# Attention into a gated feed-forward layer on one core: weights loaded in thirds, output buffers moved, more load buffers, the last output row block split

## The chip, the cores and the metric

The kernel runs on one NeuronCore of a Trainium2 chip. Its time is the device time of one execution in microseconds. Four executions of the kernel before took 388.49, 388.51, 391.55 and 392.05 us, a median of 390.03 us. A further execution was recorded by the hardware profiler; all durations below come from that one.

TensorE (PE) does the matrix products, with its weight loads listed apart as PEld. VectorE is DVE, ScalarE is ACT, GpSimd is POOL, and SyncE is SP. SP does nothing but issue DMAs here. POOL issues DMAs too, those that change the type on the way.

## The reference

```
scores = q @ k_all^T / 8          # k_all: 16 beacon keys, then 576 keys; causal on the 576
a      = softmax(scores)          # per batch (8) and head (8), 576 queries, D = 64
attn   = a @ v_all
x      = attn as [4608 tokens, 512]
out    = (relu(x @ w_gate) * (x @ w_val)) @ w_out      # d_ff = 1536, output fp32
```

## The kernel before, in words

The work is one long list of steps, written out by hand in `plan`. Instructions are emitted in program order, and each engine runs its own in that order; an instruction that waits holds up all that stand behind it on the same engine. A step of a batch takes two attention units (`Unit`): `qk` writes scores to PSUM, `exp` is done by ACT, and POOL zeroes what the causal mask removes (L353). A chunk of queries whose units are all done gets its values in the next step (`Chunk.av` on PE, `invert` and `scale` on DVE), which writes transposed rows into `xT`. Between attention pieces stands feed-forward work on 512-token tiles (`Ffn`): 12 groups `up` (four gate matmuls L420, ReLU on ACT L423, four value matmuls L429, product on DVE L431) and 4 groups `down` (12 matmuls L436, copy by ACT to an output buffer `ob` L439, and a store on SP L441 that is queued at the start of the next step).

Steps 0 to 6 are batch 0, steps 7 to 10 feed-forward alone (0, 3, 3 and 2 groups), steps 11 to 17 batch 1 with one group each, steps 18 and 19 feed-forward alone (3 groups each), and from step 20 each of batches 2 to 7 takes seven steps. In the code `s2` is 11. The groups of the first tile (four downs among them) are the 8 of steps 8 to 10, the 7 of steps 11 to 17, and the first of step 18.

PSUM has eight banks: `s_ps` two buffers of two banks (scores, and the value product of an `up` when its argument `spare` is true), `f_ps` two buffers of one bank (gate product, value product when `spare` is false, down product), `o_ps` two of one.

Queues matter around the change. POOL issues the weight loads (`load_w`, two DMAs a call), then the second batch's keys and queries (`load_cast_quarter`, eight DMAs), a tiny memset that holds back SP's loads of that batch's values, and later `w_out` in two DMAs (`load_wo`). SP issues everything else: raw fp32 tiles into the `stage` buffers (L231), transposing DMAs of cast tiles (L255) and the stores (L441). For batch 2 and on, `fetch(b, s0, late)` spreads 15 tiles (key, query, value for each of five row blocks) over steps: tile row `j` is loaded at `s0+j`, cast on POOL at `s0+j+late`, transposed by SP one step later. Batch 2 has `s0` = 11 and `late` = 3; batch 3 has `s0` = 20 and `late` = 1. Of the actions of a step, the first half is emitted before the step's feed-forward groups and before the second unit's exp and mask, the rest after them.

At the start PE runs idle matmuls on a memset tile (`warm_up`). At the end, groups left over run one after the other, and SP stores the last 128 rows.

Of the kernel before, what the change touches and what calls it, by code (L numbers as in the profile page):

```python
# [10 lines left out]
FP32 = mybir.dt.float32  # L11
BF16 = mybir.dt.bfloat16
# [141 lines left out]
def kernel(  # L154
# [23 lines left out]
    M_TILE = 512  # L178
# [4 lines left out]


    const = ctx.enter_context(tc.tile_pool(name="const", bufs=1))
    wg = const.tile([P, KM, d_ff], BF16, name="wg")
    nc.vector.memset(wg[:, 0, :M_TILE], 1.0)
    ident = const.tile([P, P], BF16, name="ident")
    make_identity(nc, ident)
    ones = const.tile([P, C], BF16, name="ones")  # L190
    nc.vector.memset(ones, 1.0)
    xT = const.tile([P, KM, n_tokens], BF16, name="xT")
    wv = const.tile([P, KM, d_ff], BF16, name="wv")
    wo = const.tile([P, NF, d_model], BF16, name="wo")
    bounds = [const.tile([P, 256], FP32, name=n) for n in ("least", "most")]
    for x in bounds:
        nc.vector.memset(x, 1.0)

    main = ctx.enter_context(ExitStack())
    kvq = main.enter_context(tc.tile_pool(name="kvq", bufs=2))  # L200
    stage = main.enter_context(tc.tile_pool(name="stage", bufs=8))
    half = main.enter_context(tc.tile_pool(name="half", bufs=6))
    psb = main.enter_context(tc.tile_pool(name="psb", bufs=10))
    nrm = main.enter_context(tc.tile_pool(name="nrm", bufs=7))
    fsb = main.enter_context(tc.tile_pool(name="fsb", bufs=2))
    osb_p = main.enter_context(tc.tile_pool(name="osb", bufs=3))
# [201 lines left out]
    class Ffn:  # L408
# [22 lines left out]
            nc.vector.tensor_mul(self.h[:, nf, c0:c1], gs[:, :n], u[:, :n])  # L431

        def down(self, ms):
            o = f_ps.tile([P, d_model], FP32, name="f")
            for nf in range(NF):
                nc.tensor.matmul(o, self.h[:, nf, ms * P:(ms + 1) * P], wo[:, nf, :],  # L436
                                 start=(nf == 0), stop=(nf == NF - 1))
            ob = osb_p.tile([P, d_model], FP32, name="ob")
            nc.scalar.copy(ob, o)  # L439
            m = self.m0 + ms * P  # L440
            later_sp.append(lambda: nc.sync.dma_start(out[m:m + P, :], ob))  # L441

        def groups(self, c0, c1, d0, d1):
            t = (c1 - c0) * 8 / 2400
# [17 lines left out]
        return cnt  # L462

    ffn_tiles = [Ffn(m * M_TILE) for m in range(n_tokens // M_TILE)]
    later_sp = []
    STEPS = 7

    ALONE = ((0, 3, 3, 2), (3, 3))
    BASE = [STEPS * b + sum(map(len, ALONE[:b])) for b in range(B)]
# [8 lines left out]
    with tc.manual_schedule():  # L478
        batches = {}
        dve, act, pool = nc.vector.tensor_copy, nc.scalar.copy, nc.gpsimd.tensor_copy  # L480
        wide_ctx = ExitStack()
# [8 lines left out]
            x.tails = [x.load_rows(k[x.b, :, 512:]), x.load_rows(q[x.b, :, 512:])]  # L490


        idle_ps = o_ps.tile([P, 256], FP32, name="os")

        def warm_up(count, n):
            for _ in range(count):
                nc.tensor.matmul(idle_ps[:, :n], wg[:, 0, :P], wg[:, 0, :n],
                                 start=True, stop=True)

        first = batches[0] = Batch(0)  # L500
# [7 lines left out]
        load_tails(first)  # L508
        for t in range(2, NKT):
            first.load("v", t)  # L510
        warm_up(8, 256)
        first.turn_rows(first.cast_rows(first.beacon, dve), first.kT[:, :, :Nb], dve)()
        warm_up(4, 256)
        def turn_first(i, g):
            for n in "kq":
                ps = f_ps.tile([P, 2, 2, P], BF16, name="f")
                first.turn_quarter(n, i, g, ps, act if n == "q" and g == 0 else dve)()
                if i == 0 and n == "k":
                    warm_up(2, P)
# [7 lines left out]
        warm_up(5, P)  # L527
        cast_first(0, 1)

        def turn_two(x, i, k_bank):  # L530
# [22 lines left out]
        def after(step, action):  # L553
            later_half.setdefault(step, []).append(action)
# [4 lines left out]
        s2 = BASE[1]  # L559

        def turn_next():
            turn_first(0, 1)
            warm_up(5, P)

        between[0] = turn_next
        mid[0] = lambda: cast_first(1, 0)
# [3 lines left out]
        def turn_last():  # L570
            turn_first(1, 0)
            ps = o_ps.tile([P, 2, 2, 2, P], BF16, name="ab")
            moves = []
            for x, n in enumerate("kq"):
                moves.append(first.turn_quarter(n, 1, 1, ps[:, x], dve))
                warm_up((8, 4)[x], P)
            for move in moves:
                move()
            cast_tails(first, dve)
# [5 lines left out]
        after(2, lambda: load_w(wv, moe_w_val, 0, 512))  # L585
        behind[3] = turn_first_tails
        after(3, lambda: first.cast("v", 4, pool))
        after(3, lambda: load_w(wg, moe_w_gate, 512, 1536))
        after(4, lambda: load_w(wv, moe_w_val, 512, 1536))

        def load_second(i):
            for g in range(2):
# [23 lines left out]
        after(s2 - 2, lambda: turn_small(second))  # L616
        mid[s2 - 1] = lambda: turn_two(second, 0, s_ps)
        between[s2 + 1] = lambda: turn_two(second, 1, f_ps)
        after(s2 + 1, wide_ctx.close)

        def fetch(b, s0, late=1):
            at(s0, lambda: batches.update({b: Batch(b)}))
            for j, u in enumerate(UNITS):
                s = s0 + j // 3
                at(s, lambda u=u: batches[b].load(*u))
                at(s + late, lambda u=u: batches[b].cast(*u, pool))
                if u[0] != "v":
                    at(s + late + 1, lambda u=u: batches[b].turn(*u))

        fetch(2, s2, 3)  # L630
        for b in range(3, B):
            fetch(b, BASE[b] - STEPS)

        spans = [(m, m + M_TILE) for m in range(0, n_tokens, M_TILE)]
# [10 lines left out]
        for s, (b, i, quota) in enumerate(plan):  # L645
            have = max([have] + [t for at_, t in ready.items() if at_ <= s])
            while spans and spans[0][1] <= have:
                t0, t1 = spans.pop(0)
                f = ffn_tiles[t0 // M_TILE]
# [53 lines left out]
            for j, (kind, _, run) in enumerate(mine):  # L703
                if j == 0 and other and (kind == "down" or len(mine) == 1):
                    other.pop().exp()
                ups = kinds.count("up")
                run((b is None and (s, j) != (s2 - 1, len(mine) - 1)) or (ups > 1 and j == (1 if ups > 2 else 0)))
                if j == 0:
                    for c in chunks if b != 1 else []:
                        c.scale()  # L710
                        notes.append(c.note)
                    if b is None and s in mid:
                        mid[s]()
                if other:
                    other.pop().exp()
                if b is None and notes:
                    notes.pop(0)()
# [65 lines left out]
```

## Time and profile before

| what | value |
|---|---|
| median of four executions | 390.03 us |
| the profiled execution's own time | 393.2 us |
| its span on the core | 391.3 us |
| PE busy, share of span | 367.7 us, 94% |
| DVE / ACT / POOL busy | 205.4 / 191.7 / 121.7 us |
| mean granted TensorE clock | 0.995 |
| PE busy from 0 to 26, 26 to 61, 61 to 84, 84 to 386 us | 18.49 of 26, 31.77 of 35, 19.53 of 23, 297.94 of 302 us |
| the same stretches, GB/s moved by DMA | 213, 192, 178, 110 |

The page of the profile divides the span into 40 slices and gives each engine's busy share in tenths. Busy time of PE is not PE at its peak, since matmuls overlap; a stretch without busy time is idle for certain. The timeline lists instructions by start, with the idle time of the engine before and what ended it. A store or load on SP shows how long SP took to issue it, not the transfer itself; the time to its landing stands in the table of DMA issues.

### The profile page before, as it was taken

The page shows a single profiled execution, that of the slowest core. Times are in us where ns is not written, and L with a number is a line of the kernel's source. Part 1 is how long each engine was busy: PE and PEld are TensorE (multiplying, and loading weights), DVE is VectorE, ACT ScalarE, POOL GpSimd, SP SyncE. Part 2 cuts the span into 40 slices and gives each one's busy share as a digit, 9 for nine tenths or more (in the row PEclk, how much of TensorE's full clock was granted, in tenths as well). Part 3 has the DMA queues.
Part 4 walks back from the last instruction along what each step waited for, and adds up shares of the span by engine and source line. Part 5 has one row for each costly group of instructions (what it writes and reads, how often), then busy time and mean ns, then how long its engine had stood idle before and what let it go on. Part 6 is the DMA issues. An engine that isn't in the chain of part 4 may idle for free.

```text
span 391.3 us, 10186 instructions
## 1 busy us (share of the span) xinstructions
PE 367.7 (94%) x4252; PEld 186.6 (48%) x4308; DVE 205.4 (53%) x333; ACT 191.7 (49%) x268; POOL 121.7 (31%) x213
## 2 busy tenths in 40 slices
PE   6768999799999999999999999999999999999994
PEld 4543555334554545445544545454545454444441
DVE  4876476345674566466447653665365644412320
ACT  4843494136655554565546545645465533313321
POOL 1882454315543442254225332334201100000000
PEclk9999999989999999999999999999999999999999
DMA  7999997958968782698258924793200020011002
GB/s 227 204 207 187 187 209 172 180 150 187 190 172 211 148 166 81 161 188 178 66 130 208 172 73 132 188 191 71 96 27 2 2 82 28 0 54 56 0 28 85
DMA packets 145555, 49.84 MB, mean 127 GB/s; under 512 B 133216, under 2 KB 139872, under 8 KB 145504
## 3 DMA queue, kind: packets, MB, share of 16 engines
q1 hardware_dynamic: 137536, 43.37, 48.1%
q0 software_dynamic: 7968, 5.77, 9.9%
q8 instruction: 35, 0.57, 0.6%
q14 instruction: 16, 0.13, 0.1%
HBM read 38.27 MB, written 9.44 MB: 122 GB/s over the span
## 4 chain that ended last, share of the span: by engine, by line
PE 85%; DMA 6%; issue 2%; ACT 2%; SPq 2%; DVE 1%; POOL 1%; ACTq 0%; DVEq 0%
PE f L436 23%; PE f L420 23%; PE s L429 13%; PE f L429 10%; PE s L337 6%; PE ab L386 6%; DMA wo<-in_moe_w_out_dram 3%; PE os L386 2%; DMA raw<-in_k_dram 1%; SPq L231 1%; ACT e L345 1%; DMA wide<-in_q_dram 1%; DMA out_dram<-ob 1%; ACT ob L439 0%; DVE r L394 0%
## 5 line engine op out<-in xcount | busy, mean ns | idle before, releaser
L420 PE MATMUL f<-xT,wg 128*128 128x512 bf16 x407 | 110.0, 382 | 5.7 <-ACT ob L439 2.8
L345 ACT ACTIVATE e<-s 128x1024 bf16<-128x1024 f32 (+2 forms) x112 | 104.3, 965 | 21.9 <-PE s L337 21.8
L423 ACT ACTIVATE g<-f 128x512 f32<-128x512 f32 x108 | 64.6, 598 | 87.7 <-PE f L420 80.9
L353 POOL TENSOR_SCALAR_AFFINE_SELECT e<-e 128x512 bf16<-128x512 bf16 (+2 forms) x80 | 47.1, 600 | 162.6 <-ACT e L345 154.0
L436 PE MATMUL f<-wo,hT 128*128 128x512 bf16 x408 | 94.7, 379 | 2.9 <-issue 1.6
L394 DVE RECIPROCAL r<-os 128x240 f32<-128x240 f32 (+2 forms) x45 | 61.0, 1355 | 39.5 <-PE os L386 39.4
L431 DVE TENSOR_TENSOR hT<-g,s 128x512 bf16<-128x512 f32 x59 | 40.5, 687 | 64.8 <-PE s L429 55.8
L429 PEld LDWEIGHTS <-wv 128*128 128x128 bf16 x432 | 42.4, 98 | 52.8 <-issue 3.0
L420 PEld LDWEIGHTS <-wg 128*128 128x128 bf16 x432 | 40.0, 98 | 52.4 <-issue 7.0
L431 DVE TENSOR_TENSOR hT<-g,f 128x512 bf16<-128x512 f32 x49 | 33.7, 688 | 57.6 <-PE f L429 51.8
L436 PEld LDWEIGHTS <-hT 128*128 128x128 bf16 x432 | 40.3, 98 | 48.1 <-issue 0.8
L429 PE MATMUL s<-xT,wv 128*128 128x512 bf16 x231 | 61.0, 383 | 0.2
L439 ACT COPY ob<-f 128x512 f32<-128x512 f32 x36 | 21.1, 587 | 77.1 <-PE f L436 62.8
L429 PE MATMUL f<-xT,wv 128*128 128x512 bf16 x195 | 50.0, 379 | 0.5 <-ACT qT L284 0.2
L250 POOL CAST half<-raw 128x512 bf16<-128x512 f32 (+2 forms) x60 | 36.4, 627 | 16.9 <-DMA kT<-half 6.7
L386 PE MATMUL ab<-e,v 128*32 128x80 bf16 (+4 forms) x1320 | 38.8, 231 | 2.5 <-issue 1.6
L337 PE MATMUL s<-qT,kT 64*128 64x80 bf16 (+3 forms) x704 | 34.0, 228 | 3.0 <-ACT e L345 1.8
L337 PEld LDWEIGHTS <-kT 64*128 64x128 bf16 x704 | 20.1, 95 | 25.8 <-issue 22.6
L386 PEld LDWEIGHTS <-v 128*32 128x32 bf16 (+1 forms) x1408 | 26.4, 97 | 11.1 <-issue 5.9
L386 PE MATMUL os<-e,ones 128*32 128x240 bf16 (+4 forms) x660 | 31.6, 230 | 0.0
L246 POOL CAST v<-raw 128x512 bf16<-128x512 f32 (+1 forms) x40 | 26.1, 656 | 9.0 <-DMA raw<-in_v_dram 8.7
L399 DVE TENSOR_TENSOR xT<-ab,r 128x480 bf16<-128x480 f32 (+2 forms) x45 | 25.0, 555 | 1.0
(59 smaller groups left out, 126.9 us busy)
## 6 DMA issues: line engine op xcount, KB each, us to landing
out_dram<-ob SPq DMA_DIRECT2D x36, 256.0 KB, 2.3
raw<-in_v_dram SPq DMA_DIRECT2D x24, 256.0 KB, 4.4
raw<-in_q_dram SPq DMA_DIRECT2D x24, 256.0 KB, 4.0
raw<-in_k_dram SPq DMA_DIRECT2D x18, 256.0 KB, 4.1
raw<-in_v_dram SPq DMA_DIRECT2D x8, 224.0 KB, 3.7
wo<-in_moe_w_out_dram POOLq DMA_DIRECT2D x2, 768.0 KB, 11.7
raw<-in_k_dram SPq DMA_DIRECT2D x6, 224.0 KB, 4.1
raw<-in_v_dram SPq DMA_DIRECT2D x8, 160.0 KB, 3.8
```

What stands on the lines that cost most here:

```text
L246: copy(self.v[:n, t].rearrange("p (h a d) -> p h a d", a=2, d=C), raw[:n].rearrange("p (h d a) -> p h a d", a=2, d=C))
L250: copy(h[:n], raw[:n])
L337: nc.tensor.matmul(self.s[:, a, c + j * n:c + (j + 1) * n], self.batch.kT[rows, 2 * g + j, kt * P:(kt + 1) * P], self.batch.qT[rows, 2 * g ...
L345: nc.scalar.activation(e[:, :k * 4 * n].rearrange("p (k a x) -> p a k x", k=k, a=2), self.s[:, :, :k * 2 * n].rearrange("p a (k x) -> p a ...
L353: nc.gpsimd.affine_select(out=cols[:, :, :m], in_=cols[:, :, :m], pattern=[[0, 4], [1, m]], compare_op=ALU.is_ge, fill=0.0, base=base, cha ...
L386: nc.tensor.matmul(o[:, q0 - cq0:q0 - cq0 + n], w, e[:kr, 2 * (hh % 2) + hh // 2], start=(i == 0 and part != 1), stop=(i == self.last), sk ...
L394: nc.vector.reciprocal(self.r[:, :n], self.os[:, :n])
L420: nc.tensor.matmul(g[:, :n], wg[:, ki, nf * P:(nf + 1) * P], x[:, ki], start=(ki == 0), stop=(ki == KM - 1))
L423: nc.scalar.activation(gs[:, :n], g[:, :n], AF.Relu)
L429: nc.tensor.matmul(u[:, :n], wv[:, ki, nf * P:(nf + 1) * P], x[:, ki], start=(ki == 0), stop=(ki == KM - 1))
L431: nc.vector.tensor_mul(self.h[:, nf, c0:c1], gs[:, :n], u[:, :n])
L436: nc.tensor.matmul(o, self.h[:, nf, ms * P:(ms + 1) * P], wo[:, nf, :], start=(nf == 0), stop=(nf == NF - 1))
```

## The change

- `wo` is allocated first and takes the place of `wg` as the memset tile that the idle matmuls read. There are fewer and wider idle matmuls: 8 of 256 columns become 4 of 512, 4 of 256 become 2 of 512, 5 of 128 become 2 of 256, and so on; 38 become 14.
- `w_gate` and `w_val` were loaded as columns 0 to 512 and 512 to 1536. They are now loaded as three parts of 512. The middle parts stay after steps 3 and 4; the last parts come after step 6, ahead of the second batch's keys and queries on POOL.
- `stage` has ten buffers instead of eight.
- The output buffers `ob` were three, in a pool of their own. They are six, in a pool made after step 12, when the pool `wide` has been closed, and they use its space.
- The last 128 output rows are computed, copied and stored in two halves of 256 columns.
- Batch 3 is fetched from step 18 with `late` = 2, instead of step 20 with `late` = 1.
- In steps of feed-forward alone the last group of each step is now run with `spare` false; before, that was so for step 10 only.

```
-    wg = const.tile([P, KM, d_ff], BF16, name="wg")
-    nc.vector.memset(wg[:, 0, :M_TILE], 1.0)
+    wo = const.tile([P, NF, d_model], BF16, name="wo")
+    nc.vector.memset(wo[:, 0], 1.0)
...
-    stage = main.enter_context(tc.tile_pool(name="stage", bufs=8))
+    stage = main.enter_context(tc.tile_pool(name="stage", bufs=10))
...
-    osb_p = main.enter_context(tc.tile_pool(name="osb", bufs=3))
...
         def down(self, ms):
-            o = f_ps.tile([P, d_model], FP32, name="f")
-            for nf in range(NF):
-                nc.tensor.matmul(o, self.h[:, nf, ms * P:(ms + 1) * P], wo[:, nf, :],
-                                 start=(nf == 0), stop=(nf == NF - 1))
-            ob = osb_p.tile([P, d_model], FP32, name="ob")
-            nc.scalar.copy(ob, o)
-            m = self.m0 + ms * P
-            later_sp.append(lambda: nc.sync.dma_start(out[m:m + P, :], ob))
+            last = self.m0 + (ms + 1) * P == n_tokens
+            for n0 in range(0, d_model, 256) if last else (0,):
+                n = slice(n0, n0 + 256) if last else slice(0, d_model)
+                o = f_ps.tile([P, d_model], FP32, name="f")
+                for nf in range(NF):
+                    nc.tensor.matmul(o[:, n], self.h[:, nf, ms * P:(ms + 1) * P], wo[:, nf, n],
+                                     start=(nf == 0), stop=(nf == NF - 1))
+                ob = pools["osb"].tile([P, d_model], FP32, name="ob")
+                nc.scalar.copy(ob[:, n], o[:, n])
+                m = self.m0 + ms * P
+                later_sp.append(
+                    lambda m=m, n=n, ob=ob: nc.sync.dma_start(out[m:m + P, n], ob[:, n]))
...
-        idle_ps = o_ps.tile([P, 256], FP32, name="os")
+        idle_ps = o_ps.tile([P, M_TILE], FP32, name="os")
...
-                nc.tensor.matmul(idle_ps[:, :n], wg[:, 0, :P], wg[:, 0, :n],
+                nc.tensor.matmul(idle_ps[:, :n], wo[:, 0, :P], wo[:, 0, :n],
...
-        after(3, lambda: load_w(wg, moe_w_gate, 512, 1536))
-        after(4, lambda: load_w(wv, moe_w_val, 512, 1536))
+        after(3, lambda: load_w(wg, moe_w_gate, 512, 1024))
+        after(4, lambda: load_w(wv, moe_w_val, 512, 1024))
+        after(6, lambda: load_w(wg, moe_w_gate, 1024, 1536))
+        after(6, lambda: load_w(wv, moe_w_val, 1024, 1536))
...
-        after(s2 + 1, wide_ctx.close)
+
+        def close_wide():
+            wide_ctx.close()
+            pools["osb"] = main.enter_context(tc.tile_pool(name="osb", bufs=6))
+
+        after(s2 + 1, close_wide)
...
         fetch(2, s2, 3)
-        for b in range(3, B):
+        fetch(3, BASE[3] - STEPS - 2, 2)
+        for b in range(4, B):
             fetch(b, BASE[b] - STEPS)
...
-                run((b is None and (s, j) != (s2 - 1, len(mine) - 1)) or (ups > 1 and j == (1 if ups > 2 else 0)))
+                run((b is None and j < len(mine) - 1) or (ups > 1 and j == (1 if ups > 2 else 0)))
```

More of the change, by code (lines that the diff above doesn't have):

```diff
@@ L192 @@
     xT = const.tile([P, KM, n_tokens], BF16, name="xT")
+    wg = const.tile([P, KM, d_ff], BF16, name="wg")
     wv = const.tile([P, KM, d_ff], BF16, name="wv")
-    wo = const.tile([P, NF, d_model], BF16, name="wo")
     bounds = [const.tile([P, 256], FP32, name=n) for n in ("least", "most")]
@@ L464 @@
     ffn_tiles = [Ffn(m * M_TILE) for m in range(n_tokens // M_TILE)]
-    later_sp = []
+    later_sp, pools = [], {}
     STEPS = 7
@@ L510 @@
             first.load("v", t)
-        warm_up(8, 256)
+        warm_up(4, M_TILE)
         first.turn_rows(first.cast_rows(first.beacon, dve), first.kT[:, :, :Nb], dve)()
-        warm_up(4, 256)
+        warm_up(2, M_TILE)
         def turn_first(i, g):
@@ L518, in turn_first @@
                 if i == 0 and n == "k":
-                    warm_up(2, P)
+                    warm_up(1, 256)
         def cast_first(i, g):
@@ L526 @@
         turn_first(0, 0)
-        warm_up(5, P)
+        warm_up(2, 256)
         cast_first(0, 1)
@@ L562, in turn_next @@
             turn_first(0, 1)
-            warm_up(5, P)
+            warm_up(2, 256)
         between[0] = turn_next
@@ L575, in turn_last @@
                 moves.append(first.turn_quarter(n, 1, 1, ps[:, x], dve))
-                warm_up((8, 4)[x], P)
+                warm_up(1, (M_TILE, 256)[x])
             for move in moves:
```

## The prediction

> **What bounds the kernel now.** I read the page's slices first, then the list of waits, then the timeline around the one place where both show a hole.
>
> ```profile
> span 391.3 us, 10186 instructions
> ...
> PE   6768999799999999999999999999999999999994
> ...
> PEclk9999999989999999999999999999999999999999
> ```
>
> PE is full from the third slice on. The two thin places are the first 26 us (attention of batch 0, where little else can run) and one slice near 76 us, followed by the only slice with a lower clock. From 84 us to 386 us PE is busy 297.94 of 302 us, so whatever is done must arrive ahead of 84 us or in the tail; between them it can only move PE's work forward as a block.
>
> ```profile
> ACT ob L439 <- DMA out_dram<-ob: 6.6, 1, 6.6
> ...
> PE f L420 <- ACT ob L439: 2.8, 1, 2.8
> ...
> PE f L436 <- DMA wo<-in_moe_w_out_dram: 0.6, 1, 0.6
> ```
>
> The hole is a full set of output buffers. The fourth copy needs the first buffer back, and its store waited on SP:
>
> ```profile
> 70.96 0.59 ACT L439 COPY ob<-f 128x512 f32<-128x512 f32 x1 [1.76 <-PE f L436]
> 78.13 0.59 ACT L439 COPY ob<-f 128x512 f32<-128x512 f32 x1 [6.58 <-DMA out_dram<-ob]
> ```
>
> The first copy ended at 63.3 us, but SP issued its store at 74.84. The queue of SP explains it:
>
> ```profile
> 71.76 1.60 SPq L231 DMA_DIRECT2D raw<-in_k_dram  x1
> ...
> 74.84 0.46 SPq L441 DMA_DIRECT2D out_dram<-ob  x1
> 75.35 1.25 SPq L255 DMA_TRANSPOSE kT<-half  x1
> ...
> 82.22 1.22 SPq L255 DMA_TRANSPOSE kT<-half  x1
> 83.53 1.21 SPq L255 DMA_TRANSPOSE qT<-half  x1
> 84.84 0.53 SPq L441 DMA_DIRECT2D out_dram<-ob  x1
> 85.46 1.21 SPq L255 DMA_TRANSPOSE kT<-half  x1
> 86.76 1.19 SPq L255 DMA_TRANSPOSE qT<-half  x1
> 88.00 0.57 SPq L231 DMA_DIRECT2D raw<-in_beacon_k_dram  x1
> ```
>
> SP hardly rests from 58 us to 95 us. Up to 69 us its loads take 0.8 to 3.3 us each to issue while DMA moves 209 and 175 GB/s (50 to 60 and 60 to 70 us); after that each transpose costs 1.2 us of issuing. So **SP's queue is a second bound, just behind PE**, and it does not depend on PE. This decides my forecast.
>
> **Part by part.**
>
> *Six output buffers.* The stall of 2.77 us at 78.76 goes: stores still leave at 74.84, 78.02, 81.60 and 84.84, but no copy needs a fifth buffer before about 105 us. With it goes the slow clock. The granted clock was 0.58 from 80 to 84 us, and four groups of four matmuls that take 0.86 us each in the chain elsewhere took 1.02, 1.42, 1.71 and 1.15: 1.86 us. The wider `spare` rule takes away 0.54 us that the second unit of step 20 waited for a score buffer. Sum on PE: 5.2 us. Without the hole, five groups of 1.73 us from 74.11 end at 82.75, where step 20 begins instead of 87.45.
>
> *What is late next.* Step 20's second unit reads queries 368 to 496 and key block 3, that is the transposes issued at 82.22 and 83.53. A transpose of queries lands 2.4 us after its issue starts (median): 85.9. Before, PE came there at 88.4 and found it done. Now PE comes at about 83.2 and waits until 85.9. Of the 5.2 us, 2.5 are left.
>
> *Batch 3 fetched two steps earlier.* This puts five SP issues (key, query, value of row block 0, with two beacon pieces) between 84.7 and the store before the transposes of block 4. They keep their durations (0.57, 0.42, 0.56, 0.82, 0.43; 3.0 us with gaps), and the value load is issued at 87.4 instead of 90.56. Block 4 is then transposed at about 88.5 to 91, in time for step 22. The casts are the trouble. In step 20 the three casts of block 0 are the first half of the step's actions, so they stand on POOL ahead of the mask of the second unit, and in step 21 PE's values need that mask. Before, no cast stood there:
>
> ```profile
> 91.35 1.23 POOL L353 TENSOR_SCALAR_AFFINE_SELECT e<-e 128x512 bf16<-128x512 bf16 x2 [1.66 <-ACT e L345]
> ```
>
> PE's values of step 21 started at 92.80, unhindered. After: a value load with a beacon lands 3.7 us after issue (median), 87.4 + 3.7 = 91.1; cast 0.66 gives 91.8, one mask 0.62 gives 92.4, PE starts at about 92.5. Gain left there: 0.3 us. The bounds of the landing: 2.3 us (the median of a store of like size) gives 91.1 for PE and a gain of 1.7; 4.9 us (the value cast that began at 95.48 in the trace, after an issue at 90.56) gives 93.7 and a loss of 0.9. I take the median, as it is for this very form of load.
>
> *Clock.* PE would idle 2.7 us before 85.9, about the length that cost 1.86 us before. But a slow stretch right after it falls into the time that PE would spend waiting for the mask, so I cost it at nothing; if it comes later than 92 us it costs up to 1.86.
> The Trainium skill (TensorE: Matmul & The Clock Gate, "What's actually happening") says the clock halves after an idle window of some 3.4 us. The trace differs: 2.77 us was enough, perhaps since other short gaps fell in the window. By the rule the shorter new idle is free; by the row it may not be.
>
> *Weights in thirds.* Four more POOL issues of 0.72 us, 2.9 us, around 24.6 to 27.5. POOL's next work other than issuing is at 43.15, where it waited 5.75 us for a load, so these hide. The order of bytes is as before. The middle third lands earlier than the wide load did, but PE had no wait for it (its fifth value product ran at 36.4 without a gap). If smaller rows move 5% slower, the 10 us of DMA they occupy become 10.5, and second-batch loads, `w_out` and then SP's queue all move 0.5 us back. I take 0; bounds -0.5 and +0.5.
> A rule speaks against it (the Trainium skill, DMA: Bandwidth & Descriptors, "Bandwidth" and "Anatomy of one DMA": batch to 1 MiB or more, about 2 us are fixed per DMA). Four more DMAs would be 8 us by that if they ran one by one. Here the 256 KB weight loads landed after 6.6 to 6.8 us and the 512 KB ones after 8.6 to 12.2, queued behind each other, so I don't add it.
>
> *Idle matmuls, ten load buffers.* PE had holes of 1.64 and 1.74 us at 24.41 and 30.33 that the profile lays to "issue". 24 fewer matmuls and weight loads shift them or may end them: 0 to -3.4 us at that place. But PE then waits at 61.23 for `w_out`, as it did for 0.57 us, and again at 85.9. Worth nothing at the end; the two waits also swallow a loss of up to 2.5 us. Load buffers: SP's list of waits has no long one for a buffer in this stretch, its loads wait for the transfer engines. Nothing, as long as SP is as busy.
>
> *Last rows in halves.* Twelve 512-column matmuls become 24 of 256: PE equal, within 0.1. The last copy falls from 0.59 to about 0.37 (ACT's 128x256 copy), 0.2 gained. The store at the end moves half the bytes; The 36 stores of 256 KB land 2.3 us after issue (median), the last of them after 3.2 us, and loads of 32 KB after 2.9, so half the size gains between 0 and 0.9 us; I take 0.4. Sum: 0.6.
>
> *Sum:* 0.3 + 0.6 = 0.9 us off the profiled 393.2 (span 391.3 and 1.9 around it): 392.3, or 0.23%. On the median of the runs shown, 390.03, this is **389.1 us**. Unknown terms (landing -1.4 to +1.2, thirds 0.5 each way, tail -0.6 to +0.4) give it 387 to 391.5.
>
> **Rivals.**
>
> *Only the transposes bind.* The value load lands in 2.3 us, or the mask is not what step 21 waits for. Then 2.5 + 0.6 = 3.1 us: 387.0. For: DMA is only 100 GB/s from 84 to 90 us, so the landing may be quick. Against: the median. 17%.
>
> *Nothing takes the place of the wait.* If SP's queue runs 3 us or more earlier (ten buffers, quieter transfers), all 5.2 + 0.6 = 5.8 us stay: 384.3. For: two SP issues took 4 and 3.3 us around 54 to 61 us, which could shrink. Against: they shrink only if `w_out` and these loads no longer compete, and the bytes are the same. 18%.
>
> *Slower: batch 3's casts hold POOL.* Place: step 20, three casts ahead of the mask. Each us by which the value load lands after 91.4 is a us of PE. It turns to a loss there from 3.99 us after issue, and over all from 4.6. At 8 us to land, which loads of 256 KB passed while `w_out` was in flight, the loss is 4.0 - 0.6, or 3.4; with a slow clock after it 5.3 us: 393.4 to 395.3. For: POOL is in order. Against: nothing as large as `w_out` moves then. 13%.
>
> *It does not do what it says.* Fourth copy still waiting, since the new pool shares space with tiles that are read late: 389.4, the tail alone. These were last read near 49 us, so 2%.
>
> **How the numbers follow.** The forecast has 50%. A measurement of this kernel can tell about 1% from no change, 3.9 us. Faster by more needs under 386.1: the second rival and a little of the first, 0.21. Slower by more, over 393.9: most of the third but not all, 0.09. Within: 0.70. The range reaches down to the case without a new wait and up to near the slow one: 384.2 to 392.8.
>
> **What would show it.** The fourth copy without a wait on a store (right for the buffers). A PE gap before the second unit of step 20, ended by a transpose landing at about 86 us. Then a PE gap before the values of step 21, ended by POOL's mask, and on POOL casts of a key, a query and a value ahead of that mask. If neither gap is there, and PE's gaps in the first 95 us sum to about 11.5 us (14.9 before, less 2.77 and 0.54), the second rival holds. The last copy should take 0.37 us. I am wrong above all if SP's queue comes to its block 3 transposes well before 82 us.

## The result and the profile after

The changed kernel takes a median of 390.83 us (34 executions, 388.66 to 393.62), the kernel before 390.23 us beside it (55 executions). The ratio is 1.0017 with a 95% interval of 1.0004 to 1.003: within 1%, and if anything 0.7 us slower, where 0.23% faster was forecast. The profiled execution of the changed kernel took 390.41 us. Two executions of the kernel before, beside the experiments below, took 435.85 and 482.07 us at a mean clock of 0.85 and 0.76; they are in a slower state and count in no ratio.

The slices of the page of the changed kernel:

```profile
span 388.7 us, 10175 instructions
...
PE   8779998988999999999999999999999999999995
...
PEclk9999999999999999999999999999999999999998
```

The slice of low clock is gone, and so is the wait for a store. The timeline of ScalarE, third and fourth copy:

```profile
71.68 0.59 ACT L441 COPY ob<-f 128x512 f32<-128x512 f32 x1 [1.76 <-PE f L438]
75.03 0.59 ACT L441 COPY ob<-f 128x512 f32<-128x512 f32 x1 [2.76 <-PE f L438]
```

The fourth copy now waits for its matmuls alone. What stands in its place is seen in the timeline of SP and then of TensorE:

```profile
81.90 1.23 SPq L254 DMA_TRANSPOSE kT<-half  x1
83.22 1.21 SPq L254 DMA_TRANSPOSE qT<-half  x1
...
86.99 0.43 SPq L230 DMA_DIRECT2D raw<-in_v_dram  x1
```

```profile
85.68 0.29 PE L336 MATMUL s<-qT,kT 64*128 64x128 bf16 x4 [1.63 <-DMA qT<-half]
...
91.70 0.29 PE L385 MATMUL ab<-e,v 128*32 128x128 bf16 x8 [1.21 <-POOL e L352]
```

TensorE stands 1.63 us for the query transpose of row block 3 (landed 85.54), and 1.21 us for the mask of step 20's second unit. POOL's timeline shows why the mask is late: it stands behind the three early casts of batch 3.

```profile
88.21 0.61 POOL L249 CAST half<-raw 128x512 bf16<-128x512 f32 x1 [2.61 <-DMA raw<-in_k_dram]
89.00 0.62 POOL L249 CAST half<-raw 128x512 bf16<-128x512 f32 x1 [0.17 <-DMA raw<-in_q_dram]
90.42 0.64 POOL L245 CAST v<-raw 128x512 bf16<-128x512 f32 x1 [0.81 <-DMA raw<-in_v_dram]
91.01 1.81 POOL L352 TENSOR_SCALAR_AFFINE_SELECT e<-e 128x512 bf16<-128x512 bf16 x3
```

So the waits that were forecast are there, in the places forecast, within about a microsecond. The question is why the time is not below that of before.

### The profile page after: what moved, and what is told of

The parts are those of the page before. It is cut to its first block, busy times and chain, and to the rows that moved or that the text cites. A ratio compares the mean times of both kernels' runs of the same rounds, so it can differ in the third digit from the quotient of the medians.

```text
span 388.7 us, 10175 instructions
## 1 busy us (share of the span) xinstructions
PE 368.5 (95%) x4239; PEld 187.4 (48%) x4296; DVE 205.6 (53%) x333; ACT 192.0 (49%) x269; POOL 124.6 (32%) x217
## 4 chain that ended last, share of the span: by engine, by line
PE 84%; DMA 6%; POOL 3%; SPq 2%; issue 2%; ACT 1%; DVE 1%; POOLq 0%; DVEq 0%; ACTq 0%
PE f L438 23%; PE f L419 22%; PE s L428 11%; PE f L428 11%; PE s L336 6%; PE ab L385 6%; DMA raw<-in_v_dram 5%; PE os L385 2%; DMA wide<-in_k_dram 1%; POOL e L352 1%; POOL v L245 1%; POOL wg L312 1%; SPq L230 1%; POOL wv L312 1%; PE f L282 1%
## 5 line engine op out<-in xcount | busy, mean ns | idle before, releaser
L438 PE MATMUL f<-wo,hT 128*128 128x512 bf16 (+1 forms) x420 | 94.8, 373 | 3.4 <-issue 1.6
L430 DVE TENSOR_TENSOR hT<-g,f 128x512 bf16<-128x512 f32 x54 | 37.1, 688 | 60.4 <-PE f L428 54.5
L430 DVE TENSOR_TENSOR hT<-g,s 128x512 bf16<-128x512 f32 x54 | 37.1, 687 | 55.7 <-PE s L428 52.6
L438 PEld LDWEIGHTS <-hT 128*128 128x128 bf16 x444 | 41.4, 98 | 47.7 <-issue 1.3
L441 ACT COPY ob<-f 128x512 f32<-128x512 f32 (+1 forms) x37 | 21.3, 575 | 73.8 <-PE f L438 73.8
L428 PE MATMUL f<-xT,wv 128*128 128x512 bf16 x213 | 55.1, 379 | 0.6 <-ACT qT L283 0.2
L428 PE MATMUL s<-xT,wv 128*128 128x512 bf16 x213 | 55.1, 379 | 0.1
L336 PE MATMUL s<-qT,kT 64*128 64x80 bf16 (+3 forms) x704 | 34.8, 231 | 3.9 <-ACT e L344 1.9
```

The costliest lines, as they stand in the source:

```text
L336: nc.tensor.matmul(self.s[:, a, c + j * n:c + (j + 1) * n], self.batch.kT[rows, 2 * g + j, kt * P:(kt + 1) * P], self.batch.qT[rows, 2 * g ...
L428: nc.tensor.matmul(u[:, :n], wv[:, ki, nf * P:(nf + 1) * P], x[:, ki], start=(ki == 0), stop=(ki == KM - 1))
L438: nc.tensor.matmul(o[:, n], self.h[:, nf, ms * P:(ms + 1) * P], wo[:, nf, n], start=(nf == 0), stop=(nf == NF - 1))
```

## The experiments

Each variant is given with the median of its own executions, twelve unless another number is named. Its ratio, with the 95% interval in brackets, is against the kernel before, run beside it on the same chip; it need not equal the quotient of two medians. Twelve executions give a ratio to within some 0.3%, that is 1.1 us, so single ratios tell little; the groups tell more.

### Each edit alone, or taken back

*Six buffers alone*, the kernel before with nothing but them:

```
-    osb_p = main.enter_context(tc.tile_pool(name="osb", bufs=3))
...
-            ob = osb_p.tile([P, d_model], FP32, name="ob")
+            ob = pools["osb"].tile([P, d_model], FP32, name="ob")
...
+            pools["osb"] = main.enter_context(tc.tile_pool(name="osb", bufs=6))
```

> The kernel before with six output buffers in the wide buffers' space and nothing else of the change. Theory (the gain of the buffers is cut by SP's queue, and the rest of it given back by batch 3's early casts on POOL): the fourth copy doesn't wait, PE reaches step 20's second unit near 83 us and waits there for the transposed queries until about 86 us, and there is no gap before the values of step 21, as no cast stands ahead of the mask. 0.5 to 2.5 us faster than before, ratio 0.994 to 0.999. Rival (the loss of the whole change sits in the first 26 us, in the fewer idle matmuls): faster by the same, so this run alone doesn't part the two. Rival (a full set of output buffers costs little in a usual execution): ratio 0.999 to 1.001.

Measured: 390.47 us, ratio 0.9998 (0.9965 to 1.0031). The stall is gone and no gain can be seen, as the rival of a small cost in a usual execution had it; 1.3 us either way lie within the interval. The timeline of TensorE shows the wait that came, and a slow clock behind it:

```profile
85.58 0.40 PE L336 MATMUL s<-qT,kT 64*128 64x128 bf16 x4 [1.80 <-DMA qT<-half]
85.91 1.89 PE L419 MATMUL f<-xT,wg 128*128 128x512 bf16 x4
87.59 1.56 PE L428 MATMUL s<-xT,wv 128*128 128x512 bf16 x4
88.98 1.03 PE L419 MATMUL f<-xT,wg 128*128 128x512 bf16 x4
```

The group at 85.91 took 1.89 us where the same takes 1.03 at 88.98.

*The changed kernel, batch 3 fetched as before* (`fetch` from step 20, `late` 1):

> The changed kernel with batch 3 fetched from step 20 with late 1, as before the change. Theory (batch 3's casts hold the mask of step 20 on POOL): the gap of 1.2 us before the values of step 21 is gone, the one of 1.6 us before the second unit of step 20 stays; 1.0 to 1.5 us faster than the changed kernel, so a ratio of 0.997 to 0.999 to before. Rivals (the loss is in the idle matmuls, or in the weights in thirds): as the changed kernel, 1.001 to 1.003.

Measured: 390.41 us, ratio 1.0026 (0.9999 to 1.0053). The mask wait is gone; the wait for the transposes is 2.40 us and has a slow stretch of 3.41 us behind it. No gain can be seen.

*The changed kernel with the 38 old idle matmuls*:

> The changed kernel with the 38 idle matmuls of before, still on the new tile. Theory (SP's queue and POOL's mask bind at 86 and 92 us, so a later start is swallowed by the waits there): as the changed kernel, ratio 1.000 to 1.003 to before. Rival (the fewer idle matmuls leave the clock low for the first 14 us, as in the profile of the changed kernel, and that is the loss): 1 to 1.7 us faster than the changed kernel, ratio 0.997 to 0.999, and a clock that rises before 8 us.

Measured: 390.61 us, ratio 1.0029 (0.9998 to 1.006): the idle matmuls are worth nothing that can be seen. The rival was that fewer of them keep the clock low for longer: the full clock was first granted at 14.38 us in the profile of the changed kernel, at 4.86 in that of the kernel before, and at 7.17 in this one, with no gain in time. Variants with the old idle matmuls had it as late as 13.56 us (six buffers alone).

*The changed kernel with the weights in two parts*:

```
-        after(3, lambda: load_w(wg, moe_w_gate, 512, 1024))
-        after(4, lambda: load_w(wv, moe_w_val, 512, 1024))
-        after(6, lambda: load_w(wg, moe_w_gate, 1024, 1536))
-        after(6, lambda: load_w(wv, moe_w_val, 1024, 1536))
+        after(3, lambda: load_w(wg, moe_w_gate, 512, 1536))
+        after(4, lambda: load_w(wv, moe_w_val, 512, 1536))
```

> The changed kernel with the weights loaded in two parts as before. Theory (thirds move the landing of the second batch's loads, of the output weights and of SP's queue by some tenths of a microsecond): 0 to 0.6 us faster than the changed kernel, ratio 1.000 to 1.002 to before. Rival (thirds cost more, by smaller rows and four more issues on POOL): 1 us or more faster than the changed kernel, ratio under 0.9995, and the second half of the output weights lands before 60 us.

Measured: 388.58 us, ratio 0.9972 (0.9943 to 1.0), 0.45% under the changed kernel. Of the three edits taken back alone, this is the one whose undoing helps. Block 3's query transpose lands at 83.70 instead of 85.54.

*The kernel before with thirds alone* is the same edit from the other side:

> The kernel before with only the weights in thirds, the last third behind step 6. Theory: twelve pieces of 256 KB with rows of 1 KB hold the transfer engines 0.7 us longer than the old mix and come in behind one another, so that second-batch loads, w_out and SP's queue all land 0.7 to 1.8 us later and the store that the fourth copy waits for moves with them: 391.0 to 392.0 us, ratio 1.002 to 1.005. Rival (the bytes are the same, so nothing moves, as the prediction took it): ratio 1.000.

Measured: 391.17 us, ratio 1.0032 (1.0005 to 1.006). *Thirds in place*, the last third directly behind the middle one, asks whether the late place or the pieces cost:

> The changed kernel with the last thirds loaded right behind the middle ones, after steps 3 and 4, instead of after step 6: the same twelve pieces, without the later place. If the number and the row size of the pieces cost: 390.8 us, ratio 1.002, weights landed near 37.4 us. If the place behind step 6 costs (POOL issues the second batch's loads behind four more issues there): 388.6, ratio 0.997, weights landed near 35.7 us.

Measured: 391.02 us, ratio 1.0019 (0.999 to 1.0048), as for the changed kernel, and the weights took 16.17 us from first to last landing, as in the late place. So the late place is not needed for the longer stream; the pieces are. The time says less, since this variant has a price of its own: POOL issues eight loads in a row, and PE waits 4.23 us at 28.70 for a mask behind them. The number of pieces and their shorter rows changed together and are not parted by any run. The DMA part of the page, POOL's queue, before and then after (packets, MB, share of 16 engines' span):

```profile
q0 software_dynamic: 7968, 5.77, 9.9%
```

```profile
q0 software_dynamic: 9056, 5.77, 10.6%
```

The same bytes go in 1,088 packets more, and take longer. Across all twenty profiles of this study the weights took, from first to last landing, 15.6 us on average in two parts (eleven profiles, 15.1 to 16.4) and 16.4 in thirds (nine, 16.1 to 16.9). `w_out` then landed at 59.6 and 61.0 us on average, and SP issued its first transpose at 66.7 and 68.4 (64.1 to 69.0 and 67.2 to 69.2). The 0.8 us grow to 1.7 us on the way through loads and queues, of which 0.3 were there at the first landing. PE meets the delay first at `w_out`: it waits for it in seven of the nine profiles in thirds (0.3 to 1.75 us) and in two of the eleven in two parts (0.36 and 0.57). In the profile of the changed kernel:

```profile
61.16 1.46 PE L438 MATMUL f<-wo,hT 128*128 128x512 bf16 x6 [1.05 <-DMA wo<-in_moe_w_out_dram]
```

*Both taken back*, two parts and the old fetch:

> The changed kernel with the weights in two parts and batch 3 fetched as before; the other edits stay. Theory (SP's queue sets when step 20's second unit can run, thirds push that queue back, and the early casts put the mask behind them): the query transpose of row block 3 lands near 83.7 us, as with two parts alone, PE waits about 2 us for it and not at all for the mask of step 21 (1.40 us with two parts alone). 387.2 us without a slow-clock stretch behind the first wait, 388.9 with one; ratio to before 0.993 to 0.998. Rival (the early fetch costs nothing, since the mask wait only takes the place of something else): 388.6, ratio 0.997, as with two parts alone.

Measured: 389.37 us, ratio 0.997 (0.9946 to 0.9994). As with two parts alone; the early fetch is worth nothing that can be seen. Against the same kernel in thirds (old fetch, 1.0026), two parts gain 2.2 us.

### Is SP's queue the bound?

*Stores held*: the first three stores of tile 0 go behind block 3's transposes.

```
             acts = later.pop(s, [])
-            run_sp()
+            if s not in (16, 17, 18):
+                run_sp()
```

> The changed kernel, with the first three stores of tile 0 held back on SP until behind the transposes of row block 3 (six output buffers allow it). Theory: three issues of about 0.5 us and their gaps leave SP ahead of those transposes, which are issued 1.6 us earlier and land near 83.9 us; PE's wait of 1.63 us at 85.7 goes, and the value load of batch 3 and the mask behind it come earlier by as much. 389.2 us, ratio to before 0.998 (0.4% below the changed kernel). Rival (the wait only moves to the next thing, block 4's transposes behind four stores, or the mask): 390.8, ratio 1.002.

Measured: 389.83 us, ratio 0.9996 (0.997 to 1.0022). The transpose landed at 83.52, PE's wait fell from 1.63 to 0.87 us, the mask wait stayed (1.42), and one of 1.06 us for a mask came at 107.37. *The same on six buffers alone*:

> The kernel before with six output buffers in the wide buffers' space and the first three stores of tile 0 held back on SP; nothing else changed. Buffers alone gave ratio 0.9998. Theory (the gain of the buffers is eaten by PE's wait for the transposes of row block 3 and what follows it): those land 1.6 us earlier, and the ratio falls to 0.995 to 0.997. Rival (the gain of the buffers was lost elsewhere or never there): 1.000.

Measured: 388.91 us, ratio 0.9985 (0.9952 to 1.0019). There is no wait for block 3 any more, but one of 1.27 us at 112.56 for a query transpose of batch 3. *Two parts, old fetch and held stores*:

> The changed kernel with the weights in two parts, batch 3 fetched as before and the first three stores of tile 0 held back on SP. Theory (SP's queue is what is late next, and all that shortens it ahead of row block 3 counts): block 3's query transpose lands near 82.5 us instead of 84.4, PE's wait of 1.85 us falls under 0.5 us, no mask wait: 387.8 us, ratio to before 0.994. Rival (held stores gain nothing, as the interval with the early fetch still allows): ratio 0.997.

Measured: 389.83 us, ratio 1.0003 (0.9978 to 1.0028). The theory fell: the wait near 84 us was gone, but the time was not lower than with two parts and old fetch. SP's and then TensorE's timeline of this run show the next wait, with a slow stretch of 3.41 us behind it:

```profile
109.33 1.28 SPq L254 DMA_TRANSPOSE kT<-half  x1
110.70 1.21 SPq L254 DMA_TRANSPOSE qT<-half  x1
```

```profile
113.16 0.29 PE L336 MATMUL s<-qT,kT 64*128 64x128 bf16 x4 [1.86 <-DMA qT<-half]
```

In these two profiles PE loses part of what it won ahead of 113 us with the late fetch: it meets SP's queue twice. *The wait filled*: the old fetch and two parts, with seven idle matmuls ahead of the waiting scores, to keep the clock up.

> Two-part weights and old fetch as in the run of that name, and seven idle matmuls of 512 columns (1.5 us at full clock) ahead of the second unit's scores of step 20, where PE waits 1.85 us for the transposes. If a half-clock stretch behind that wait costs the executions that have it about 1.4 us (5 of 12 had a mean clock of 0.996 or less): none has it, the mean clocks rise to 0.998 or more, and the ratio falls from 0.997 to 0.994 or 0.996. Rival (the clock there costs nothing, since a later wait swallows it, or the idle matmuls push the scores back): 0.997 to 1.000.

Measured: 389.6 us, ratio 1.0005 (0.998 to 1.003), mean clock of the executions 0.997 as without them. The profiled execution had its transposes early and no wait there. This run settles nothing on the price of the slow clock.

*Nine more issues on SP*, in the kernel before and in the changed one: tile 0's first three stores cut into four of 32 rows.

```
+            for p in range(0, P, P // 4 if self.m0 == 0 and ms < 3 else P):
+                r = P // 4 if self.m0 == 0 and ms < 3 else P
+                later_sp.append(lambda p=p, r=r: nc.sync.dma_start(out[m + p:m + p + r, :], ob[p:p + r]))
```

> The kernel before, with each of the first three stores of tile 0 cut into four of 32 rows: nine issues more on SP, about 0.4 us each, ahead of row block 3's transposes; the bytes and all else stay. Theory (SP's queue sets when step 20 runs, in this kernel just as in the changed one): the fourth copy waits 1 us longer, block 3's query transpose lands near 87 to 89 us instead of 83.1 to 85.9, PE waits for it, and the time is 1.5 to 3 us longer: ratio 1.004 to 1.008. Rival (PE is ahead of nothing there, SP has slack): ratio under 1.002, and the transposes land late without anyone waiting.

> The changed kernel with the same nine issues more. Theory: PE already waits for these transposes, so nearly the whole 3 to 3.6 us come on top: query transpose lands near 88.5 us, 393.5 to 394.5 us, ratio to before 1.009 to 1.012. Rival (the six buffers make the queue harmless): 391, ratio 1.002 to 1.004.

Measured, with four executions each: 395.2 us, ratio 1.013 (1.0081 to 1.0179) for the kernel before; 395.41 us, 1.0141 (1.0093 to 1.019) for the changed one. The kernel before, SP and then TensorE:

```profile
72.01 1.86 SPq L443 DMA_DIRECT2D out_dram<-ob  x4
...
84.77 1.21 SPq L255 DMA_TRANSPOSE qT<-half  x1
```

```profile
75.94 1.02 PE L420 MATMUL f<-xT,wg 128*128 128x512 bf16 x4 [0.56 <-ACT ob L439]
...
87.25 0.40 PE L337 MATMUL s<-qT,kT 64*128 64x128 bf16 x4 [3.11 <-DMA qT<-half]
87.58 1.89 PE L420 MATMUL f<-xT,wg 128*128 128x512 bf16 x4
```

And the changed kernel, TensorE:

```profile
89.51 0.40 PE L336 MATMUL s<-qT,kT 64*128 64x128 bf16 x4 [6.98 <-DMA qT<-half]
89.84 1.89 PE L419 MATMUL f<-xT,wg 128*128 128x512 bf16 x4
```

Some 4 us of issues (three groups of four take 1.9 us each instead of 0.5) cost 5.1 us before and, against 1.0017, 4.8 us after. Both ratios exceed what was written down. Behind both waits the clock was low for 6.83 us, which likely makes the difference: in the kernel before, three groups of four matmuls took 5.1 us there instead of 2.6. The wait on PE is for block 3's transposes in both kernels. **With six buffers SP's queue sets step 20; with three it is close to it**: as it stands, the kernel before does not wait there, and its transposes landed 2.5 us ahead of their use in the first profile, 0.6 and 0.7 us in two others (see the table below).

### What further profiles of both kernels show

> The kernel before, unchanged, for a second profile of it. If the slow-clock stretch after the full set of output buffers is what the first profile had beyond a usual execution, this one has the hole of about 2.7 us near 78 us without the half clock, and a span near 388.5 us. Rival (the hole and the half clock belong together, and the 3 us lie elsewhere): both are there again, and milestones ahead of the hole differ from the first profile's (first up 26.66 us, w_out landed 56.14 and 61.19, block 3's query transpose landed 85.86).

> The kernel before, for a third profile. Theory (the full set of output buffers costs 0.4 us when SP's first store goes out early, 2.8 and more when late): the hole is between 0.4 and 2.8 us, and follows the time at which the first store is issued (72.09 us gave 0.40, 74.84 gave 2.77). Rival (the size of the hole depends on something else): no such relation.

> The changed kernel, for a second profile. Theory: PE's wait ahead of step 20's second unit follows the landing of row block 3's query transpose (85.54 us gave 1.63) and is near zero where that lands by 83.5 us; the values of step 21 then wait for the mask by 1.2 us or more. Rival: a wait of the same 1.6 us wherever the transpose lands.

| us | before, first profile | second | third | after, first | second |
|---|---|---|---|---|---|
| time of that execution | 393.2 | 388.89 | 389.64 | 390.41 | 390.46 |
| SP issues the first transpose | 68.95 | 66.64 | 66.26 | 69.24 | 68.50 |
| first store issued | 74.84 | 72.09 | 71.85 | 74.37 | 74.40 |
| hole at the fourth copy | 2.77 | 0.40 | 1.54 | none | none |
| slow clock behind it | 3.41 | none | none | none | none |
| block 3's query transpose landed | 85.86 | 83.12 | 82.87 | 85.54 | 85.31 |
| PE's wait for it | none | none | none | 1.63 | 2.13 |
| step 20's scores from it start | 88.36 | 83.69 | 83.56 | 85.68 | 85.44 |
| PE's wait for the mask in step 21 | none | none | none | 1.21 | 1.48 |
| step 21's values that need the mask start | 93.11 | 88.44 | 88.31 | 91.70 | 91.73 |
| last matmul ends | 385.69 | 381.30 | 381.56 | 384.25 | 384.33 |
| from there to the span's end | 5.59 | 5.75 | 6.15 | 4.45 | 4.43 |

The second profile of the kernel before, SP, ScalarE and TensorE:

```profile
72.09 0.46 SPq L441 DMA_DIRECT2D out_dram<-ob  x1
...
80.80 1.21 SPq L255 DMA_TRANSPOSE qT<-half  x1
```

```profile
70.34 0.58 ACT L439 COPY ob<-f 128x512 f32<-128x512 f32 x1 [1.76 <-PE f L436]
75.14 0.58 ACT L439 COPY ob<-f 128x512 f32<-128x512 f32 x1 [4.21 <-DMA out_dram<-ob]
```

```profile
75.78 1.02 PE L420 MATMUL f<-xT,wg 128*128 128x512 bf16 x4 [0.40 <-ACT ob L439]
...
83.69 0.40 PE L337 MATMUL s<-qT,kT 64*128 64x128 bf16 x8 [0.54 <-DVE hT L431]
```

The copy still waits for its store, but the store goes out 2.75 us earlier, and PE hardly stands. So the 2.77 us and the slow clock belong to the first profiled execution: it took 393.2 us, where six sets of executions of this kernel, 184 in all, have medians of 389.6 to 390.8. The size of the hole does not follow the first store alone: 71.85 gave 1.54 and 72.09 gave 0.40, because PE itself came 1.3 us earlier in the third profile. It is the race of the two that sets it. With thirds alone the store left at 74.14 us, and the hole was back: 2.48 us, with a slow stretch of 3.41 us behind it. In the changed kernel the rival of a fixed wait falls too, by little: a landing 0.23 us earlier went with a wait 0.5 us longer, since PE had come 0.7 us earlier.

### Taking the mask's wait away

*Casts behind the mask*, with the early fetch kept:

```
-                at(s + late, lambda u=u: batches[b].cast(*u, pool))
+                (after if b == 3 else at)(s + late, lambda u=u: batches[b].cast(*u, pool))
```

> The changed kernel with batch 3's casts emitted at the end of their steps, behind the second unit's mask; batch 3 is still fetched from step 18. Theory (the wait of 1.2 to 1.5 us for the mask ahead of step 21's values is the price of the early fetch, and nothing later takes its place, since early fetching also takes away the wait near 113 us that the late-fetching kernels show): no wait there, 1.2 to 1.5 us less than the changed kernel, ratio to before 0.998. Rival (the wait turns up again for batch 3's transposes, now cast later): 1.002.

Measured: 390.18 us, ratio 0.9999 (0.9975 to 1.0024). POOL's and TensorE's timelines:

```profile
88.34 1.23 POOL L352 TENSOR_SCALAR_AFFINE_SELECT e<-e 128x512 bf16<-128x512 bf16 x2 [3.51 <-ACT e L344]
89.51 1.17 POOL L249 CAST half<-raw 128x512 bf16<-128x512 f32 x2
90.62 0.64 POOL L245 CAST v<-raw 128x512 bf16<-128x512 f32 x1
```

```profile
85.47 0.29 PE L336 MATMUL s<-qT,kT 64*128 64x128 bf16 x4 [2.19 <-DMA qT<-half]
...
90.11 0.28 PE L385 MATMUL ab<-e,v 128*32 128x128 bf16 x8
```

The mask now goes first, and the value product runs at 90.11 with no wait. PE's last matmul ends 1.2 us earlier than in the changed kernel; the ratio falls by 0.0018, some 0.7 us, which the intervals can't tell from nothing. *All three costs taken off* (casts behind, two parts, stores held):

> The same with the weights in two parts and the first three stores of tile 0 held back, so that each of the three costs found is taken off the changed kernel: thirds about 1.5 us, the wait for row block 3's transposes 1.7 to 2.1 us (of which the two-part weights take a part already), the mask 1.3 us. Theory: PE stands in neither place near 85 and 91 us nor at 113, 386.5 to 387.5 us, ratio 0.991 to 0.994. Rival (a further wait on SP's queue stands right behind, as holding stores with the late fetch showed at 113 us): 0.997.

Measured: 389.78 us, ratio 0.9983 (0.9964 to 1.0002). In the profile PE has no wait over 0.45 us between 27 and 104 us and one of 0.62 us up to 125, as the theory asked, and its last matmul ends at 380.88; but the gain forecast, 0.6 to 0.9%, is not there. In the two further profiles of the kernel before it ends at 381.30 and 381.56: in such an execution little is left to win ahead of the tail. The tail was 5.42 us in this profile, against 5.75 and 6.15 there.

The two lowest ratios, 0.9972 and 0.997, are of variants with the weights in two parts, but three more of these were at 1.0003, 1.0005 and 0.9983. All five average 0.9987; the changed kernel and its five variants in thirds, leaving out the one with more issues, average 1.0014. That puts thirds at some 1.1 us, though the variants differ in more than the weights.

## Why the prediction was wrong

**Six output buffers: seen as forecast, sized from the wrong execution.** The step read "Sum on PE: 5.2 us". The stall and the slow clock were those of one execution 3 us above the median. In two others the hole was 0.40 and 1.54 us, without a slow clock. With the 0.54 us for the score buffer (0.54 in those too) the step was worth 0.9 and 2.1 us there. The warning lay in the table of times: 393.2 beside a median of 390.0. The forecast scaled the sum to the median and did not ask which term the excess was in. So the 0.3 us that the sum kept at step 21 had the wrong starting point: the values that need the mask ran 1.4 us earlier after the change than in the first profile, but 3.3 us later than in the two others.

**What is late next: right.** PE waits for block 3's transposes, landing at 85.54 (85.9 forecast), in the changed kernel and in most variants, and nine issues more on SP moved both kernels by 5 us. But the number was right by luck: that timetable was the late one of the first profile. In the two others of the kernel before they landed at 83.12 and 82.87. Over all profiles without held stores or added issues they landed at 81.7 to 85.9 with two parts (seven, average 83.9) and at 84.5 to 86.0 in thirds (seven, average 85.3), so thirds made the late timetable the usual one.

**Weights in thirds: the term of the sum that failed.** It was taken at 0, with bounds of 0.5 either way. Measured: 1.2 us added alone (1.0032); 1.7 us gained back when undone (1.0017 to 0.9972), 2.2 with the old fetch (1.0026 to 0.997). The prediction weighed rows that move 5% slower, over the 10 us of the wide loads alone. The whole stream of 15.6 us became 0.8 us, or 5%, longer, so the share was right and the stretch too short. The path named as the danger (second-batch loads, `w_out`, SP's queue) is the one it took; along it the delay grew to 1.7 us, and PE had no slack there. The forecast was 0.9 us faster, the result 0.7 us slower; this term has the size of that miss. The rule of the Trainium skill that spoke against more DMAs (DMA: Bandwidth & Descriptors, "Bandwidth" and "Anatomy of one DMA") had the sign right; of the 8 us estimated from its fixed cost, this case shows 0.8 us in the stream.

**Batch 3's casts: right.** Three casts ahead of the mask, PE's values at 91.70 (92.5 forecast), and with the casts behind the mask the wait was gone. The value load landed 3.3 us after its issue (3.7 forecast). The upper bound of 4.9 us was misread: that cast stood behind two others on POOL, and its load had landed after 4.33 us. The rivals that needed no new wait, and the one of 8 us to land, did not happen.

**Idle matmuls and the clock.** Nothing from the first, as forecast. A slow stretch behind the new wait was costed at nothing. In both profiles of the changed kernel there was none, in the second by luck of where the gap fell (see the last section); in three of its variants there was one. The guess that other short gaps added to the 2.77 us is not borne out: the hole itself made PE idle for 2.22 of the 3.41 us that counted.

**Last rows in halves: under-sized.** 0.6 us forecast. From the last matmul to the end the kernel before takes 5.59, 5.75 and 6.15 us, the changed one 4.45 and 4.43. Over all profiles the tail averages 5.8 us with the whole store (seven) and 4.8 in halves (thirteen): 1.0 us. The copy took 0.37 us as forecast,

```profile
384.29 0.37 ACT L441 COPY ob<-f 128x256 f32<-128x256 f32 x1 [0.94 <-PE f L438]
```

and the last store landed 1.8 us after its issue began, where the whole one took 3.2 and 3.75 in two profiles of the kernel before. Where its landing is on record it took 2.2 us on average in halves (eleven profiles) and 3.3 whole (five): 1.0 us, not 0.4.

By the runs the balance is: thirds +1.1 to +2.2, tail -1.0, buffers alone -0.1, fetch and idle matmuls about 0; what rests on ratios is known to about 1.1 us at best. That leaves 0 to +1.1 against the +0.7 measured: it fits within those errors, no closer.

## What to carry to other kernels

When the profiled execution is 3 us above the median, find out which of its waits the median doesn't have before counting one as gain; a second profile costs little and here it changed the largest term. Where PE runs just ahead of or just behind a queue, work added to that queue costs (here 5 us for nine issues), and what is won at one meeting point can be lost at the next one (here 85 us, 91 us, 113 us). Count a transfer cut into more pieces as a delay for everything queued behind it, and follow that delay to the place where PE meets the queue.

## What was not expected of the hardware

An idle TensorE of 1.6 to 2.4 us may or may not cost clock. Gaps of 1.80, 1.86, 2.35 and 2.40 us were followed by a half-clock stretch of 3.41 us, gaps of 1.63, 1.76, 1.85, 2.13 and 2.19 were not; 2.48 and 2.77 were, and 3.11, 4.23 and 6.98 by one of 6.83.

By the traces it matters how much of a gap falls into one and the same window. In each of the twenty profiles all changes of the granted clock lie whole multiples of 3.413 us apart, whether or not PE had gaps in between: in the first profile of the kernel before at 4.86, 79.95, 83.37 and 390.57 us, that is 22, 1 and 90 times 3.413. So the clock is set window by window, and a gap does not start a window. Laid on these windows:

| profile | gap, us | windows it falls in, us | PE busy in each | clock behind each |
|---|---|---|---|---|
| kernel before, first | 2.77 | 73.13 to 76.54, to 79.95 | 84%, 35% | 1.00, 0.50 |
| six buffers alone | 1.80 | 81.83 to 85.24, to 88.65 | 41%, 90% | 0.50, 1.00 |
| changed kernel, first | 1.63 | 82.65 to 86.06 | 50% | 1.00 |
| changed kernel, second | 2.13 | 81.02 to 84.43, to 87.84 | 66%, 70% | 1.00, 1.00 |
| casts behind the mask | 2.19 | 80.86 to 84.27, to 87.69 | 69%, 65% | 1.00, 1.00 |

In the last two a window's edge cut the gap about in half, and it cost no clock; with six buffers alone a second gap of 0.54 us fell into the first window. Between 20 and 375 us the clock fell nine times in all profiles together, each time behind a window in which PE was busy for at most 46%. Of the other windows at full clock there one was busy for 44%, all the rest for 48% or more. Some matmul records are missing from the traces (56 of 4308 in the first), so the shares are good to some hundredths, and a short stretch without a record need not be idle. This is read from the traces; no run moved a gap across an edge on purpose. In the first 20 us the clock also fell behind windows that were busy for 59 to 69%. The Trainium skill (TensorE: Matmul & The Clock Gate, "What's actually happening") tells of a free-running window of some 3.4 us: the traces agree with it. That a whole window must be idle does not hold here.

Whether such a stretch shows in the time is not settled. Locally it cost the first profile 1.7 to 1.9 us of PE. For executions without a profile only the mean clock is known, and it doesn't tell where the clock was low: one stretch of 3.41 us takes about 0.004 off it (half of 3.41 in 390), but so does the low clock behind the last matmul in the third profile of the kernel before, and a stretch in the first 20 us does the same. Of 127 executions of the kernel before, 20 with 0.999 averaged 389.9 us, 30 with 0.996 389.6, 13 with 0.993 or 0.994 391.4, and 9 with 0.989 to 0.992 389.8, which is no steady relation. Of the three profiles of the kernel before one had a slow stretch in the middle; how many of the other executions had one is not known.
